# One-core attention and MLP-mixer kernel: ScalarE, VectorE and GpSimd put in written order beside TensorE, and the float64 weight conversion rearranged

## The chip, the cores and the metric

The kernel runs on one core of one Trainium2 chip. The core has five engines with an instruction stream each: PE (TensorE, matrix products), DVE (VectorE), ACT (ScalarE), POOL (GpSimd) and SP (SyncE, which here only issues DMAs). Each works through its stream in order and waits on semaphores for the others. The metric is the device time of one execution, in microseconds (us).

## The reference, cut to what matters

```
q, k, v: (8, 12, 448, 64) float32;  w_tok1 (448, 256), w_tok2 (256, 448), w_ch1 (768, 1536), w_ch2 (1536, 768) float64
q_n, k_n = rmsnorm(q, g_q), rmsnorm(k, g_k)
x  = softmax(q_n k_n^T / 8) v                    # per batch and head, then heads side by side: (8, 448, 768)
u  = x + (relu(x^T w_tok1) w_tok2)^T
out = u + relu(u w_ch1) w_ch2
```

The four weights arrive as float64. No engine operation used here reads float64, so the kernel loads each number as two 32-bit words and builds the float32 value itself.

## The kernel before, in words

Work goes by head pairs: 8 batches of 6 pairs, 48 in all. An attention step is half a pair: `score` (4 products of 448 columns into the four `s_ps` buffers, 4 exponentials on ACT that write `e`), `av` of the step before, and in the first half of a pair `denominator` of the pair before (a product with `one_c`, then transpose `dt`, reciprocal `rc`, transpose `rd`, product `uT` on DVE). `chunk_sums` adds up `e` over the keys: on POOL in a pair's first half, two additions on DVE in its second. `norm_pair` (square on ACT, `ms` on DVE, the power `rs` on POOL) and `scale` (POOL) prepare the pair two ahead; `trans_qk` (PE transposes, ACT eviction to `qkT`) the pair one ahead; `load_qk` loads three ahead.

The MLP of a batch is `trans_x`, `tok1`, `tok2`, `ch1`, `ch2`, `trans_y`. All its products, the transposes and the denominators share the two PSUM buffers of `m_ps`. The tiles `x` and `y` share one buffer, so the first `x` of a batch waits until the output DMA of the batch before has read `y`.

A weight chunk is 256 columns of 128 (or 112) rows of float64; there are 8 of the token weights, 36 of w_ch1 and 36 of w_ch2, 80 in all. Its conversion, by the lines of the profile: `raw` is loaded (L129, SP); DVE cuts out exponent (L151, to `e_t`) and mantissa (L152, to `m_t`); POOL clamps and rebases the exponent in two operations (L154, L155); ACT makes the mantissa a number (L156); DVE adds the low word (L172) and the sign (L174); POOL multiplies the two into the weight (L176, `wc_sb` or `w_sb`).

`merge` interleaves lists of items by their costs. The first stretch of the program holds 14 attention steps (the seven pairs 0 to 6) with chunk items 0 to 14. Then comes a stretch for each batch: its MLP merged with 12 attention steps of the batch after, and in the stretch of batch 0 also chunk items 15 to 80. The first stretch is called A here, that of batch 0 B. The last batch has no attention beside it.

Only PE runs in the order in which this program writes its instructions. The streams of the other engines are ordered by a scheduler, which may move an instruction ahead of others that are written before it.

Of the kernel before, what the change touches and what calls it, by code (L numbers as in the profile page):

```python
# [8 lines left out]
F32 = mybir.dt.float32  # L9
# [3 lines left out]
AF = mybir.ActivationFunctionType  # L13
ALU = mybir.AluOpType
# [26 lines left out]
def whole(ctx, tc, shifted, pre, q, k, v, g_q, g_k, moe_w_tok1, moe_w_tok2, moe_w_ch1, moe_w_ch2, out):  # L41


    nc = tc.nc
    ctx.enter_context(tc.manual_schedule(engines={nc.tensor.engine}))

    B, H, S, D = q.shape
    C = H * D
# [14 lines left out]
    SCALE = 1.0 / float(D) ** 0.5  # L63
# [18 lines left out]
    ident, one_c = pre.ident, pre.one_c
    g_t = const.tile([P, 2], F32, name="g_t")
    for i, g in enumerate((g_q, g_k)):
        for a in range(2):
            nc.scalar.dma_start(out=g_t[a * D:(a + 1) * D, i:i + 1], in_=g.rearrange("(p o) -> p o", o=1))
    nc.vector.tensor_scalar(g_t[:, 0:1], g_t[:, 0:1], SCALE, None, ALU.mult)
# [36 lines left out]
    def weight_load(i):  # L124
        rows, src, dst, split = chunks[i]
        n = src.shape[-1]
        if src.dtype == I64:
            t = raw_pool.tile([P, WCOLS, 2], U32, name="raw")
            nc.sync.dma_start(  # L129
                out=t[0:rows, 0:n, :].rearrange("p n w -> p (n w)"), in_=src.bitcast(U32))  # L130
            st["raw", i] = t
        elif split:
            t = raw_pool.tile([P, WCOLS], F32, name="raw")
            nc.sync.dma_start(out=t[0:rows, 0:n], in_=src)
            st["raw", i] = t
        else:
            nc.sync.dma_start(out=dst, in_=src)

    def convert_first(i):

        rows, src, dst, split = chunks[i]
        n = src.shape[-1]
        if src.dtype != I64:
            return
        hi = st["raw", i][0:rows, 0:n, 1]
        e_t = cv_pool.tile([P, WCOLS], U32, name="e_t")
        m_t = cv_pool.tile([P, WCOLS], U32, name="m_t")
        st["cv", i] = e_t, m_t
        e, m = e_t[0:rows, 0:n], m_t[0:rows, 0:n]
        ef, mf = e.bitcast(F32), m.bitcast(F32)  # L150
        nc.vector.tensor_scalar(e, hi, 0x7FF00000, None, ALU.bitwise_and)  # L151
        nc.vector.tensor_scalar(m, hi, 0x000FFFFF, None, ALU.bitwise_and)  # L152

        nc.gpsimd.tensor_scalar(ef, e, 1151.0 * 2**20, 896.0 * 2**20, ALU.min, ALU.max)  # L154
        nc.gpsimd.tensor_scalar(e, ef, -896.0 * 2**20, 8.0, ALU.add, ALU.mult)  # L155
        nc.scalar.activation(out=mf, in_=m, func=AF.Identity, bias=one_c[0:rows, 0:1], scale=2.0**-20)  # L156

    def convert_last(i):
# [16 lines left out]
            out=e, in0=hi, scalar=0x80000000, in1=e, op0=ALU.bitwise_and, op1=ALU.bitwise_or)  # L175
        nc.gpsimd.tensor_tensor(out=dst, in0=fold(mf), in1=fold(ef), op=ALU.mult)  # L176

    LOADS_AHEAD = 2

    def weight_items(lo, hi):  # L180

        def one(i):
            if i + LOADS_AHEAD < len(chunks):
                weight_load(i + LOADS_AHEAD)
            if i < len(chunks):
                convert_first(i)
# [302 lines left out]
class Start:  # L489


    def __init__(self, ctx, tc, q, k):
# [33 lines left out]

    def norm_pair(self, p, st, apart=False):
# [6 lines left out]
        st["rs", p] = rs = self.st_pool.tile([128, 2 * n], F32, name="rs")  # L534
# [15 lines left out]
def kernel(  # L550
# [29 lines left out]
    pre = Start(ctx, tc, q, k)  # L580
# [35 lines left out]
```

## Time and profile before

| | us |
|---|---|
| median of 3 runs | 1734.93 (1734.03 to 1735.23) |
| the profiled execution, its own time | 1736.05 |
| its span in the trace | 1734.2 |
| PE busy (matrix products) | 1558.9, 90% of the span |
| DVE busy | 490.7, 28% |
| ACT busy | 465.0, 27% |
| POOL busy | 447.6, 26% |

The span runs from the first instruction to the last; 1.85 us of the execution lie around it. Busy shares are means over the whole span, and the stretches A and B differ from the rest, so the rows further down are taken by stretch.

### The profile page before, as it was taken

The page shows a single profiled execution, that of the slowest core. Times are in us where ns is not written, and L with a number is a line of the kernel's source. Part 1 is how long each engine was busy: PE and PEld are TensorE (multiplying, and loading weights), DVE is VectorE, ACT ScalarE, POOL GpSimd, SP SyncE. Part 2 cuts the span into 40 slices and gives each one's busy share as a digit, 9 for nine tenths or more (in the row PEclk, how much of TensorE's full clock was granted, in tenths as well). Part 3 has the DMA queues.
Part 4 walks back from the last instruction along what each step waited for, and adds up shares of the span by engine and source line. Part 5 has one row for each costly group of instructions (what it writes and reads, how often), then busy time and mean ns, then how long its engine had stood idle before and what let it go on. Part 6 is the DMA issues. An engine that isn't in the chain of part 4 may idle for free.

```text
span 1734.2 us, 13947 instructions
## 1 busy us (share of the span) xinstructions
PE 1558.9 (90%) x5248; PEld 740.4 (43%) x5248; DVE 490.7 (28%) x831; ACT 465.0 (27%) x810; POOL 447.6 (26%) x393
## 2 busy tenths in 40 slices
PE   5576659999999899998999899998999989998998
PEld 2223224444444444444444444444444444444554
DVE  5867893212212221222122221122212221111000
ACT  4453333222222223222222222222222222221000
POOL 7878883111211111211121112121112111200000
PEclk8778979999999899998999999998999989999999
DMA  4333431020001100111100200011010111001001
GB/s 115 99 106 98 114 113 28 16 54 21 22 16 43 33 21 24 26 32 32 27 22 16 59 20 18 21 43 32 16 27 22 32 32 27 22 1 32 0 0 33
DMA packets 119889, 65.76 MB, mean 38 GB/s; under 512 B 91716, under 2 KB 109892, under 8 KB 119812
## 3 DMA queue, kind: packets, MB, share of 16 engines
q1 hardware_dynamic: 112066, 53.76, 11.9%
q10 hardware_dynamic: 7746, 11.01, 2.1%
q8 instruction: 43, 0.70, 0.2%
q14 instruction: 34, 0.28, 0.1%
HBM read 53.74 MB, written 11.01 MB: 37 GB/s over the span
## 4 chain that ended last, share of the span: by engine, by line
PE 79%; POOL 6%; DVE 6%; DMA 3%; ACT 2%; issue 2%; SPq 1%; ACTq 0%; DVEq 0%; POOLq 0%
PE m_ps L419 26%; PE m_ps L406 25%; PE s_ps L231 8%; PE o_ps L288 8%; PE m_ps L382 5%; PE m_ps L390 4%; DMA qk<-in_k_dram 2%; PE m_ps L302 2%; PE m_ps L216 2%; POOL rs L544 1%; POOL wc_sb L176 1%; SPq L524 1%; POOL e_t L154 1%; DMA raw<-in_moe_w_ch_dram 1%; DVE uT L424 1%
## 5 line engine op out<-in xcount | busy, mean ns | idle before, releaser
L406 PE MATMUL m_ps<-uT,wc_sb 128*128 128x448 f32 x1152 | 452.9, 547 | 26.9 <-ACT h L410 17.3
L419 PE MATMUL m_ps<-h,wc_sb 128*128 128x448 f32 x1152 | 452.4, 544 | 6.7 <-DVE uT L424 5.5
L544 POOL TENSOR_TENSOR rs<-ms,mhalf_c 112x16 f32<-112x16 f32 (+1 forms) x49 | 140.4, 2866 | 981.2 <-DVE ms L543 980.6
L406 PEld LDWEIGHTS m_ps<-uT,wc_sb 128*128 128x128 f32 x1152 | 215.5, 191 | 248.0 <-issue 206.9
L419 PEld LDWEIGHTS m_ps<-h,wc_sb 128*128 128x128 f32 x1152 | 212.8, 190 | 220.1 <-issue 207.0
L237 ACT ACTIVATE e<-s_ps,rs 112x448 f32<-112x448 f32 x384 | 213.5, 633 | 177.7 <-PE s_ps L231 174.5
L231 PE MATMUL s_ps<-qkT 64*112 64x448 f32 x768 | 184.1, 594 | 16.5 <-ACT qkT L218 11.6
L278 DVE TENSOR_TENSOR es<-es,e 112x896 f32<-112x896 f32 x96 | 105.5, 1099 | 287.8 <-ACT e L237 283.8
L288 PE MATMUL o_ps<-e,vt 112*64 112x448 f32 x768 | 171.1, 568 | 0.0
L539 DVE TENSOR_REDUCE ms<-sq 112x16 f32<-112x1024 f32 (+1 forms) x49 | 58.5, 1196 | 293.2 <-ACT sq L536 293.2
L410 ACT ACTIVATE h<-m_ps 128x448 f32<-128x448 f32 x96 | 51.9, 541 | 308.0 <-PE m_ps L406 308.0
L218 ACT ACTIVATE qkT<-m_ps,g_t 128x448 f32<-128x448 f32 x96 | 60.6, 633 | 221.7 <-PE m_ps L216 217.9
L274 POOL TENSOR_TENSOR es<-e 112x896 f32<-112x896 f32 x48 | 100.2, 2087 | 73.9 <-PE m_ps L302 73.3
L424 DVE TENSOR_TENSOR uT<-uT,m_ps 128x448 f32<-128x448 f32 x48 | 29.8, 620 | 309.3 <-PE m_ps L419 309.3
L231 PEld LDWEIGHTS s_ps<-qkT 64*112 64x112 f32 x768 | 65.7, 182 | 116.8 <-issue 89.0
L382 PE MATMUL m_ps<-x,w_sb 112*128 112x384 f32 x256 | 97.7, 540 | 10.0 <-DVE dt L314 9.5
L216 PE MATMUL m_ps<-ident,qk 112*128 112x112 f32 x384 | 57.1, 278 | 49.5 <-POOL qk L207 40.7
L288 PEld LDWEIGHTS o_ps<-e,vt 112*64 112x64 f32 x768 | 47.9, 140 | 116.0 <-issue 114.7
L390 PE MATMUL m_ps<-w_sb,h 128*128 128x448 f32 x192 | 79.8, 558 | 12.2 <-DVE uT L395 12.2
L433 ACT COPY y<-m_ps 112x512 f32<-112x512 f32 x48 | 28.0, 586 | 221.9 <-PE m_ps L431 221.9
L536 ACT ACTIVATE sq<-qk 112x1024 f32<-112x1024 f32 (+1 forms) x49 | 50.7, 1037 | 119.7 <-DMA qk<-in_k_dram 118.5
L216 PEld LDWEIGHTS m_ps<-ident,qk 112*128 112x128 f32 x384 | 46.3, 150 | 84.8 <-issue 38.9
(41 smaller groups left out, 873.1 us busy)
## 6 DMA issues: line engine op xcount, KB each, us to landing
raw<-in_moe_w_ch_dram SPq DMA_DIRECT2D x72, 256.0 KB, 2.8
qk<-in_q_dram SPq DMA_DIRECT2D x96, 112.0 KB, 2.8
qk<-in_k_dram SPq DMA_DIRECT2D x96, 112.0 KB, 2.9
vt<-in_v_dram SPq DMA_DIRECT2D x48, 224.0 KB, 2.6
out_dram<-y ACTq DMA_DIRECT2D x16, 672.0 KB, 4.6
raw<-in_moe_w_tok_dram SPq DMA_DIRECT2D x4, 224.0 KB, 4.3
raw<-in_moe_w_tok_dram SPq DMA_DIRECT2D x2, 256.0 KB, 2.6
raw<-in_moe_w_tok_dram SPq DMA_DIRECT2D x2, 192.0 KB, 2.3
```

The lines of the kernel that those rows point to most:

```text
L216: nc.tensor.transpose(ps[:, c * R:(c + 1) * R], qk[0:R, i, c].rearrange("p h d -> p (h d)"), ident[0:R, 0:R])
L218: nc.scalar.mul(st["qkT", p][:, i, :], ps[:, 0:S], g_t[:, i:i + 1])
L231: nc.tensor.matmul(out=ps[0:R, 0:S], lhsT=qkT[a * D:(a + 1) * D, 1, kc * R:(kc + 1) * R], rhs=qkT[a * D:(a + 1) * D, 0, :], start=True, st ...
L237: nc.scalar.activation(out=e[0:R, a, i, :], in_=pss[a][0:R, 0:S], func=AF.Exp, scale=st["rs", p][0:R, r:r + 1])
L274: nc.gpsimd.tensor_tensor(out=es[0:R], in0=e[0:R, :, 0, :], in1=e[0:R, :, 1, :], op=ALU.add)
L278: nc.vector.tensor_tensor(out=es[0:R], in0=es[0:R], in1=e[0:R, :, i, :], op=ALU.add)
L288: nc.tensor.matmul(out=o[a * D:(a + 1) * D, 0:S], lhsT=vt[0:R, a, kc * D:(kc + 1) * D], rhs=e[0:R, a, i, :], start=(kc == 0), stop=(kc == ...
L382: nc.tensor.matmul(out=ps[:, 0:HC], lhsT=w1_sb[0:R, c, jc * P:(jc + 1) * P], rhs=st["x"][0:R, c, cs], start=(c == 0), stop=(c == NS - 1))
L390: nc.tensor.matmul(out=ps[:, 0:S], lhsT=st["h1", jc][:, cc * P:(cc + 1) * P], rhs=w2_sb[:, jc].rearrange("p c r -> p (c r)"), start=(jc == ...
L406: nc.tensor.matmul(out=ps[:, 0:S], lhsT=wc1_sb[:, cc, f * P:(f + 1) * P], rhs=st["uT", b][:, cc, :], start=(cc == 0), stop=(cc == NC - 1))
L419: nc.tensor.matmul(out=ps[:, 0:S], lhsT=wc2_sb[:, f, cc * P:(cc + 1) * P], rhs=st["h2"][:, f, :], start=(f == 0), stop=(f == NF - 1))
L544: nc.gpsimd.tensor_tensor(out=rs[0:R, w], in0=ms[0:R, w], in1=self.mhalf_c[0:R].to_broadcast([R, (hi - lo) * n]), op=ALU.pow)
```

## The change

All four compute engines are put in written order. The clamp and rebasing of the exponent, two POOL operations, become one ACT operation, `Relu(8 x + bias)` with the bias from `expo_c`; ACT has it ahead of the mantissa's operation. In a chunk's item the load now stands last and fetches three chunks ahead instead of two. `chunk_sums` becomes an item of its own, with cost 1.0, after the step's products. The q and k of pairs 0 and 1 are loaded into the buffer that later takes w_ch2 (`wc2_sb`), so the three buffers of `qk_pool` start with pair 2; the k of pair 0 is issued on ACT's queue instead of SP's; the gains `g_t` are loaded and scaled before the branch.

```diff
-    ctx.enter_context(tc.manual_schedule(engines={nc.tensor.engine}))
+    ctx.enter_context(tc.manual_schedule(engines={
+        e.engine for e in (nc.tensor, nc.vector, nc.scalar, nc.gpsimd)}))
...
-        nc.gpsimd.tensor_scalar(ef, e, 1151.0 * 2**20, 896.0 * 2**20, ALU.min, ALU.max)
-        nc.gpsimd.tensor_scalar(e, ef, -896.0 * 2**20, 8.0, ALU.add, ALU.mult)
+        nc.scalar.activation(out=e, in_=e, func=AF.Relu, bias=expo_c[0:rows, 0:1], scale=8.0)
         nc.scalar.activation(out=mf, in_=m, func=AF.Identity, bias=one_c[0:rows, 0:1], scale=2.0**-20)
...
-    LOADS_AHEAD = 2
+    LOADS_AHEAD = 3
...
         def one(i):
-            if i + LOADS_AHEAD < len(chunks):
-                weight_load(i + LOADS_AHEAD)
             if i < len(chunks):
                 convert_first(i)
             if i:
                 convert_last(i - 1)
+            if i + LOADS_AHEAD < len(chunks):
+                weight_load(i + LOADS_AHEAD)
...
                 (score_shifted if shifted else score)(p, h)
-                chunk_sums(p, h)
...
-        items.append((4.4 - 0.8 * h, tiled))
+        items.append((3.4 - 0.8 * h, tiled))
+        if g < NG:
+            items.append((1.0, lambda: chunk_sums(p, h)))
...
+        self.wc2_sb = const.tile([P, NF, C], F32, name="wc2_sb")
+        flat = self.wc2_sb[:].rearrange("p f c -> p (f c)")
+        for p in range(2):
+            self.st["qk", p] = flat[:, 2 * p * n:2 * (p + 1) * n].rearrange(
+                "p (i c h d) -> p i c h d", i=2, c=self.NS, h=2)
-        self.load_qk(0, self.st)
+        self.load_qk(0, self.st, other=nc.scalar)
         self.load_qk(1, self.st)
```

How the streams move is shown at two places. The first is ACT in stretch A, one head pair. `e` is an exponential, `sq` the square of `norm_pair`, `qkT` the eviction of the transposes; `m_t` and `e_t` belong to a chunk. Before:

```order
L237 ACTIVATE e<-s_ps,rs 112x448
L156 ACTIVATE m_t<-m_t,one_c 128x256
L237 ACTIVATE e<-s_ps,rs 112x448 x3
L536 ACTIVATE sq<-qk 112x1024
L156 ACTIVATE m_t<-m_t,one_c 128x256
L237 ACTIVATE e<-s_ps,rs 112x448 x3
L156 ACTIVATE m_t<-m_t,one_c 128x256
L237 ACTIVATE e<-s_ps,rs 112x448
L218 ACTIVATE qkT<-m_ps,g_t 128x448 x2
L156 ACTIVATE m_t<-m_t,one_c 128x256
```

After:

```order
L233 ACTIVATE e<-s_ps,rs 112x448 x4
L553 ACTIVATE sq<-qk 112x1024
L151 ACTIVATE e_t<-e_t,expo_c 128x192
L152 ACTIVATE m_t<-m_t,one_c 128x192
L233 ACTIVATE e<-s_ps,rs 112x448 x4
L214 ACTIVATE qkT<-m_ps,g_t 128x448 x2
L151 ACTIVATE e_t<-e_t,expo_c 128x256
L152 ACTIVATE m_t<-m_t,one_c 128x256
```

The four exponentials of a step now stand together, a pair has two chunks in place of about four, and a chunk has two ACT operations that follow each other.

The same place on DVE, after the change; `es` are the additions of `chunk_sums`, `dt` to `uT` the denominator, `ms` of `norm_pair`.

```order
L274 TENSOR_TENSOR es<-es,e 112x896 x2
L148 TENSOR_SCALAR e_t<-raw 128x256
L149 TENSOR_SCALAR m_t<-raw 128x256
L168 SCALAR_TENSOR_TENSOR m_t<-raw,m_t 128x192
L170 SCALAR_TENSOR_TENSOR e_t<-raw,e_t 128x192
L310 STREAM_TRANSPOSE dt<-m_ps 128x448
L312 RECIPROCAL rc<-dt 128x14
L314 STREAM_TRANSPOSE rd<-rc 128x448
L316 TENSOR_TENSOR uT<-o_ps,rd 128x448
L556 TENSOR_REDUCE ms<-sq 112x16
L560 TENSOR_SCALAR ms<-ms 112x16
```

Before, the rows of a pair there mix about four chunks between the same attention rows:

```order
L539 TENSOR_REDUCE ms<-sq 112x16
L314 STREAM_TRANSPOSE dt<-m_ps 128x448
L543 TENSOR_SCALAR ms<-ms 112x16
L151 TENSOR_SCALAR e_t<-raw 128x256
L316 RECIPROCAL rc<-dt 128x14
L152 TENSOR_SCALAR m_t<-raw 128x256
L318 STREAM_TRANSPOSE rd<-rc 128x448
L278 TENSOR_TENSOR es<-es,e 112x896
L320 TENSOR_TENSOR uT<-o_ps,rd 128x448
L278 TENSOR_TENSOR es<-es,e 112x896
```

A chunk's first two operations now stand behind the additions, or behind the denominator and `ms`, that are written ahead of them.

The second place is POOL in stretch B. `rs` is the power, `qk` the scaling. Before:

```order
L544 TENSOR_TENSOR rs<-ms,mhalf_c 112x16
L155 TENSOR_SCALAR e_t<-e_t 128x256
L207 TENSOR_TENSOR qk<-qk,rs 112x512
L176 TENSOR_TENSOR wc_sb<-m_t,e_t 128x256
L154 TENSOR_SCALAR e_t<-e_t 128x256
L155 TENSOR_SCALAR e_t<-e_t 128x256
L176 TENSOR_TENSOR wc_sb<-m_t,e_t 128x256
L154 TENSOR_SCALAR e_t<-e_t 128x256
L155 TENSOR_SCALAR e_t<-e_t 128x256
```

After:

```order
L561 TENSOR_TENSOR rs<-ms,mhalf_c 112x16
L203 TENSOR_TENSOR qk<-qk,rs 112x512
L172 TENSOR_TENSOR wc_sb<-m_t,e_t 128x256 x11
L270 TENSOR_TENSOR es<-e 112x896
L172 TENSOR_TENSOR wc_sb<-m_t,e_t 128x256 x2
```

Of a chunk only the product is left on POOL, and a pair of stretch B has 12 or 13 of them.

## Rows read from the trace of the kernel before

**Rows 1.** Busy time by engine in stretches: start, A, B in two parts, two later batches
```profile
core 0: us, PE busy (x) PEld busy (x) DVE busy (x) ACT busy (x) POOL busy (x), PEclk, DMA share, GB/s
0.00:12.80 12.80, 0.00 (x0) 0.01 (x1) 3.20 (x11) 3.49 (x4) 5.08 (x11) 1.00 0.64 144
12.80:140.40 127.60, 83.01 (x305) 32.63 (x305) 89.82 (x184) 60.67 (x110) 106.00 (x119) 0.77 0.35 99
140.40:265.30 124.90, 80.85 (x255) 37.75 (x255) 105.06 (x214) 44.42 (x86) 106.61 (x149) 0.83 0.39 110
265.30:386.20 120.90, 118.19 (x404) 55.85 (x402) 25.90 (x38) 30.91 (x54) 24.14 (x13) 1.00 0.10 25
386.20:586.50 200.30, 190.18 (x657) 90.66 (x657) 43.50 (x63) 53.26 (x91) 35.93 (x18) 0.98 0.11 28
...
1189.60:1390.90 201.30, 191.77 (x659) 91.25 (x657) 43.69 (x63) 53.41 (x91) 35.94 (x18) 0.97 0.11 28
```

**Rows 2.** The chain that ended last, one pair of A: start, length, what
```profile
108.80 0.62 SPq L524
109.52 3.43 DMA raw<-in_moe_w_ch_dram
...
119.81 2.46 POOL qk L207
```

**Rows 3.** PE's timeline, end of A: start, length, operation, [idle before, releaser]
```profile
105.02 1.76 PE L216 MATMUL m_ps<-ident,qk 112*128 112x112 f32 x8 [5.05 <-POOL qk L207]
...
122.31 1.62 PE L216 MATMUL m_ps<-ident,qk 112*128 112x112 f32 x8 [5.00 <-POOL qk L207]
124.66 3.33 PE L231 MATMUL s_ps<-qkT 64*112 64x448 f32 x8 [0.73 <-ACT qkT L218]
...
130.15 0.92 PE L302 MATMUL m_ps<-es,one_c 112*64 112x448 f32 x4
131.00 1.76 PE L231 MATMUL s_ps<-qkT 64*112 64x448 f32 x8
132.69 1.72 PE L288 MATMUL o_ps<-e,vt 112*64 112x448 f32 x8
```

**Rows 4.** Groups by line in 0:260 us: a chunk's operations on POOL and ACT
```profile
L176 POOL TENSOR_TENSOR wc_sb<-m_t,e_t 128x256 f32<-128x256 f32 x69 | 59.3, 862 | 15.2 <-DVE e_t L174 10.5 <-DVE m_t L172 1.1
...
L154 POOL TENSOR_SCALAR e_t<-e_t 128x256 f32<-128x256 uint32 x72 | 40.5, 563 | 11.4 <-DVE e_t L151 6.1
...
L156 ACT ACTIVATE m_t<-m_t,one_c 128x256 f32<-128x256 uint32 x72 | 36.5, 507 | 94.1 <-DVE m_t L152 93.2
...
L155 POOL TENSOR_SCALAR e_t<-e_t 128x256 uint32<-128x256 f32 x72 | 34.7, 482 | 6.0
```

**Rows 5.** Groups by line, 600:1000 us, two later batches: attention's operations
```profile
L237 ACT ACTIVATE e<-s_ps,rs 112x448 f32<-112x448 f32 x96 | 52.9, 635 | 47.9 <-PE s_ps L231 47.9
...
L278 DVE TENSOR_TENSOR es<-es,e 112x896 f32<-112x896 f32 x24 | 26.2, 1092 | 90.8 <-ACT e L237 89.6
...
L218 ACT ACTIVATE qkT<-m_ps,g_t 128x448 f32<-128x448 f32 x24 | 15.2, 633 | 61.3 <-PE m_ps L216 61.3
L539 DVE TENSOR_REDUCE ms<-sq 112x16 f32<-112x1024 f32 x12 | 14.6, 1220 | 90.7 <-ACT sq L536 90.7
...
L536 ACT ACTIVATE sq<-qk 112x1024 f32<-112x1024 f32 x12 | 12.7, 1055 | 39.6 <-DMA qk<-in_k_dram 39.6
...
L314 DVE STREAM_TRANSPOSE dt<-m_ps 128x448 f32<-128x448 f32 x12 | 7.8, 650 | 35.8 <-PE m_ps L302 35.8
```

**Rows 6.** DVE's timeline in A: two of a chunk's four operations, undisturbed
```profile
85.33 0.41 DVE L174 SCALAR_TENSOR_TENSOR e_t<-raw,e_t 128x256 uint32<-128x256 uint32 x1
85.66 0.28 DVE L151 TENSOR_SCALAR e_t<-raw 128x256 uint32<-128x256 uint32 x1
```

**Rows 7.** The scaling's group in 600:1000 us
```profile
L207 POOL TENSOR_TENSOR qk<-qk,rs 112x512 f32<-112x512 f32 x12 | 12.5, 1042 | 0.9
```

**Rows 8.** Waits in 600:1000 us: total us, times, longest
```profile
PE m_ps L367 <- DVE x L374: 11.5, 4, 5.3
```

More of the change, by code (lines that the diff above doesn't have):

```diff
@@ L62, in whole @@
     assert DT % P == 0 and C % P == 0 and DC % P == 0 and HC <= 512 and S <= 512
-    SCALE = 1.0 / float(D) ** 0.5
     pool = lambda name, bufs, **kw: ctx.enter_context(tc.tile_pool(name=name, bufs=bufs, **kw))
@@ L68, in whole @@
     cv_pool = pool("cv_pool", 3)
+    pre.qk_pool = pool("qk_pool", 3)
+    pre.sq_pool = pool("sq_pool", 1)
+    pre.st_pool = pool("st_pool", 4)
     v_pool = pool("v_pool", 2)
@@ L80, in whole @@
     ps_M = pool("ps_M", 2, space=PSUM)
[L82 to L87, printed above, removed]
+    ident, one_c, expo_c, g_t = pre.ident, pre.one_c, pre.expo_c, pre.g_t
     w1_sb = const.tile([P, NS, DT], F32, name="w1_sb")
@@ L91, in whole @@
     wc1_sb = const.tile([P, NC, DC], F32, name="wc1_sb")
-    wc2_sb = const.tile([P, NF, C], F32, name="wc2_sb")
+    wc2_sb = pre.wc2_sb
     st = dict(pre.st)
@@ L149, in convert_first @@
         e, m = e_t[0:rows, 0:n], m_t[0:rows, 0:n]
-        ef, mf = e.bitcast(F32), m.bitcast(F32)
+        mf = m.bitcast(F32)
         nc.vector.tensor_scalar(e, hi, 0x7FF00000, None, ALU.bitwise_and)
         nc.vector.tensor_scalar(m, hi, 0x000FFFFF, None, ALU.bitwise_and)
-        nc.gpsimd.tensor_scalar(ef, e, 1151.0 * 2**20, 896.0 * 2**20, ALU.min, ALU.max)
-        nc.gpsimd.tensor_scalar(e, ef, -896.0 * 2**20, 8.0, ALU.add, ALU.mult)
+        nc.scalar.activation(out=e, in_=e, func=AF.Relu, bias=expo_c[0:rows, 0:1], scale=8.0)
         nc.scalar.activation(out=mf, in_=m, func=AF.Identity, bias=one_c[0:rows, 0:1], scale=2.0**-20)
@@ L489, with __init__ @@
 class Start:
-    def __init__(self, ctx, tc, q, k):
+    def __init__(self, ctx, tc, q, k, g_q, g_k, w2):
         self.nc = nc = tc.nc
@@ L500, in __init__ @@
         const = pool("start", 1)
-        self.qk_pool = pool("qk_pool", 3)
-        self.sq_pool = pool("sq_pool", 1)
-        self.st_pool = pool("st_pool", 4)
+        NF, C = w2.shape[0] // P, w2.shape[1]
+        self.wc2_sb = const.tile([P, NF, C], F32, name="wc2_sb")
+        n = 2 * self.NS * D
+        flat = self.wc2_sb[:].rearrange("p f c -> p (f c)")
+        assert NF * C >= 4 * n
         self.st = {}
-        self.load_qk(0, self.st)
+        for p in range(2):
+            self.st["qk", p] = flat[:, 2 * p * n:2 * (p + 1) * n].rearrange(
+                "p (i c h d) -> p i c h d", i=2, c=self.NS, h=2)
+        self.load_qk(0, self.st, other=nc.scalar)
         self.load_qk(1, self.st)
+        self.g_t = const.tile([P, 2], F32, name="g_t")
+        for i, g in enumerate((g_q, g_k)):
+            for a in range(2):
+                nc.scalar.dma_start(
+                    out=self.g_t[a * D:(a + 1) * D, i:i + 1], in_=g.rearrange("(p o) -> p o", o=1))
         self.mhalf_c = const.tile([P, 1], F32, name="mhalf_c")
         nc.gpsimd.memset(self.mhalf_c[:], -0.5)
-        self.norm_pair(0, self.st, apart=True)
         self.ident = const.tile([P, P], F32, name="ident")
@@ L513, in __init__ @@
         nc.gpsimd.memset(self.one_c[:], 1.0)
+        self.expo_c = const.tile([P, 1], F32, name="expo_c")
+        nc.gpsimd.memset(self.expo_c[:], -896.0 * 2**23)
+        self.st["rs", 0] = const.tile([P, 4 * self.NS], F32, name="rs_0")
+        with tc.tile_pool(name="sq_0", bufs=1) as self.sq_pool, tc.tile_pool(name="st_0", bufs=1) as self.st_pool:
+            self.norm_pair(0, self.st, apart=True)
+        nc.vector.tensor_scalar(self.g_t[:, 0:1], self.g_t[:, 0:1], 1.0 / float(D) ** 0.5, None, ALU.mult)
     def heads(self, p):
@@ L517, in heads, with load_qk @@
         return b, slice(2 * j, 2 * j + 2)
-    def load_qk(self, p, st):
+    def load_qk(self, p, st, other=None):
         b, hs = self.heads(p)
-        st["qk", p] = qk = self.qk_pool.tile([128, 2, self.NS, 2, self.D], F32, name="qk")
+        if ("qk", p) not in st:
+            st["qk", p] = self.qk_pool.tile([128, 2, self.NS, 2, self.D], F32, name="qk")
+        qk = st["qk", p]
         for i, src in enumerate((self.q, self.k)):
             for a in range(2):
-                self.nc.sync.dma_start(
+                (other if other and i else self.nc.sync).dma_start(
                     out=qk[0:self.R, i, :, a], in_=src[b, hs][a].rearrange("(p c) d -> p c d", c=self.NS))
@@ L533, in norm_pair @@
         ms = self.st_pool.tile([128, 2 * n], F32, name="ms")
-        st["rs", p] = rs = self.st_pool.tile([128, 2 * n], F32, name="rs")
+        if ("rs", p) not in st:
+            st["rs", p] = self.st_pool.tile([128, 2 * n], F32, name="rs")
+        rs = st["rs", p]
         for lo, hi in ((0, 1), (1, 2)) if apart else ((0, 2),):
@@ L579 @@
     nc.vector.tensor_scalar(small[:], most[:], SCORE_BOUND**2 / D, None, ALU.is_le)
-    pre = Start(ctx, tc, q, k)
+    pre = Start(ctx, tc, q, k, g_q, g_k, moe_w_ch2)
     with tc.If(nc.values_load(small[0:1, 0:1], min_val=0, max_val=1,
```

## The prediction

> **What bounds the kernel now.** I read the busy times by stretch first [rows 1]. In the five later batches (200.3 to 201.3 us, the first and last are shown) PE is busy for 190.2 to 191.8 us: they are bound by PE, and about 6 of the remaining 10 us are the wait of `trans_x` for the output DMA, 11.5 us in two batches [rows 8]. The first 265 us are different. PE is busy for 83.0 of 127.6 us in A and 80.9 of 124.9 us in the first part of B, at a granted clock of 0.77 and 0.83, while POOL is busy for 106.0 and 106.6 us. From 265.3 us on, with the conversions done, B runs like a later batch (118.2 of 120.9 us, clock 1.00). So there are some 90 us in which PE doesn't work, and more in which it works at the lower of its two levels (1.2 in place of 2.4 GHz), all before 265 us.
>
> The chain of waits shows what a pair of A waits for: a `raw` DMA of 3.43 us, behind it on SP's queue the q and k of a later pair (0.62 us an issue), then `ms`, the power and the scaling on POOL (2.46 us) [rows 2]; PE gets its next transposes after 5.0 us of idling for `qk`, 17.3 us after those of the pair before [rows 3]. The scheduler has put about four chunks into each pair of A, and SP, which issues in order, reaches the q and k only when the chunks ahead have given their `raw` buffers back. In B, POOL alone carries 1.91 us a chunk (0.86 + 0.56 + 0.48 [rows 4]).
>
> **Stretch A after the change.** It keeps 14 steps and has 15 chunk items, as written: two chunks a pair, not four. The loads of q and k stand behind at most one raw load each and find the three buffers of the pool empty at first, so they come a pair early; I cost them at nothing, covered by a whole pair's time (without that cover the price is the present chain, a rival below). What is left is the engines' own work and the order. ACT has, per pair, 8 exponentials of 0.635, a square of 1.06, two evictions of 0.63 [rows 5] and 2.14 chunks with two operations of about 0.51 (the new `Relu` is on the same 128x256, so I price it as L156 [rows 4]): 5.1 + 1.1 + 1.3 + 2.2 = 9.6 us. PE at full clock has 2 x (1.76 + 1.72) + 0.92 + 1.6 = 9.5 us [rows 3]. POOL has a sixth of a later batch's 35.9 us, 6.0 [rows 1], and 2.14 products of 0.86: 7.8 us.
>
> The written order adds a loop between ACT and DVE. Half 0: four exponentials (2.5), the square (1.06), on DVE `ms` (1.22) and the first cut of a chunk (0.28 [rows 6]), then on ACT the chunk's two operations (1.0): 6.1 us. Until then the next step's exponentials, whose scores are ready, stand behind the chunk on ACT. Half 1: four exponentials (2.5), the second addition (1.09) while ACT evicts `qkT` (1.27), the cut (0.28), the chunk's two (1.0): 4.9 us. Together 11.0 us, some six handoffs between engines on top; the denominator (two transposes of 0.65 and two shorter operations) ran before that unless PE was late. PE idles in this loop, so a part of its work will run at the lower clock (the same scores took 3.33 us after 5 us of idling, 1.76 us later [rows 3]) and move the denominator into the loop. I take 12.5 us a pair, from 9.6 (ACT alone) to 17.3 (as now). A then ends at 12.8 + 7 x 12.5 = 100.3 us instead of 140.4 us.
>
> The start stays at 12.8 us [rows 1]: q of pair 0 is issued first on SP as now; k leaves on ACT's queue, which saves two issues of 0.62 us [rows 2] to a transfer that isn't needed before the second half of the square. I take 0, with 1.2 us either way.
>
> **Stretch B after the change.** It has the instructions of a later batch plus 65 chunks. PE's share is that of a later batch, 201 us less the 6 us for the output DMA (batch 0 has no `y` ahead of it): 195 us. The others beside it, each as in a later batch plus 65 chunks: DVE 43.6 + 65 x 1.38 (2 x 0.28 + 2 x 0.41 [rows 6]) = 133 us; ACT 53.3 + 65 x 1.02 = 119 us; POOL 35.9 + 65 x 0.86 = 92 us. None reaches 195 us. POOL's 65 x 1.05 = 68 us of L154 and L155 are gone; ACT pays 33 us for it, beside PE's work. The DMA has to bring 105 GB/s or so in B, against 110 GB/s at a share of 0.39 now [rows 1]; no price.
>
> What the order costs in B: an eviction that PE waits for (`uT` on DVE, `h` on ACT) can stand behind one chunk's operations, 1.4 or 1.0 us. A group of `ch1` or `ch2` gives the other `m_ps` buffer enough time; the six short groups of `tok2` don't. Also, w_ch2 chunks are now converted only just before the `ch2` columns that read them, where the scheduler had finished all 80 by 265 us; at the first, third and fifth column group PE may wait for a chunk that is one or two items late. Nothing in the trace shows this. From below it is 0; from above 30 us, if DVE's and POOL's work don't overlap at all (next part). I take 11 us, nearer to 0, since every engine alone has a third of B free. B takes 206 us and ends at 306.3 us.
>
> Why an overlap could fail: the scaling takes 2.46 us in A, where DVE is busy 70% of the time [rows 1, 2], and 1.04 us in later batches [rows 7]. The Trainium skill, page "GPSIMD Engine Reference", section "1. Specifications", says why: GpSimd shares its SBUF interfaces with VectorE and contends with instructions of two SBUF inputs or in a two-port mode. By the row only the scaling is stretched, and B stays at 206 us; by the page taken as full exclusion, B would be 236 us. The trace agrees with contention; it doesn't show exclusion.
>
> **Later batches and the end.** Their instructions stay, in another order. PE's idle time there is 10 us a batch, 6 of them the output DMA, so no order can win more than 4 us a batch; what it can lose is the last rival. I take 0.
>
> **Sum.** B now ends at 386.2 us [rows 1], then at 306.3 us: 79.9 us less. Against the profiled execution's own time, 1736.05 - 79.9 = 1656 us. That execution lies 1.1 us above the median of the runs shown, so the median should be **1655 us**.
>
> **The rivals.**
> *DVE and POOL exclude each other* (that page's rule in full). For it: the stretched scaling. Against: in A now, 89.8 + 106.0 us of the two fit into 127.6 us [rows 1], though part of that is waiting inside the operations. B = 133 + 92 + 11 = 236 us, 30 more: 1685 us. 14%.
> *A stays at its pace*: the loads come late again, or the ACT and DVE loop with the slow clock reaches 17.3 us a pair. For it: the new waits stand in order. Against: half the chunks and no raw queue. A ends at 133.9 us, 34 more: 1689 us. 13%.
> *All of it is hidden*: A goes at ACT's 9.6 us, B at 195 us: 80 + 195 = 275 us, 31 less: 1624 us. For it: no engine's sum is over PE's in B. Against: the loop in A. 11%.
> *Slower*: in each of the 72 steps of the later batches DVE holds the denominator and the additions (1.3 and 2.2 us [rows 5]) or ACT its four exponentials ahead of an eviction that PE needs. From 1.1 us a step on (79.9 / 72) the gain is gone; at 2.2 us the time is 1813 us. For it: two `m_ps` buffers only. Against: the scheduler's order there already holds whole groups of four exponentials and two additions, and PE loses under 4 us a batch. 5%.
> *No effect*: the gain of A and B is eaten by conversion waits at `ch2` to within 0.2%: 3%.
>
> **How the numbers follow.** My forecast has 54%: 12.5 us a pair by about 1.5 and B's cost between 0 and 20 us give 1637 to 1673 us by themselves. The range takes in the two rivals above it at 1685 and 1689 us with a margin, and leaves out most of the hidden case, the slower one and no effect: 1635 to 1698 us. Within 0.2% (3.5 us, about what a measurement of this kernel can tell from no change) lies 3%; slower 5%; faster 92%.
>
> **What would show it.** In the trace after: no POOL line between the scaling and the product of a chunk; PE's transposes in A every 11 to 14 us; `trans_x` of batch 0 at about 100 us and that of batch 1 at about 306 us; granted clock over 0.9 through B; the later batches at 200 to 202 us. I am wrong if the batches move by more than 2 us each, if PE in B waits over 20 us for `wc_sb`, or if the power or scaling of a pair still ends A's chain.

## The result, and the profile after

The changed kernel took 1678.42 us (median, 1674.74 to 1678.93) where the kernel before took 1734.48 us beside it: a ratio of 0.9673 [0.9656, 0.969], 56 us faster, where 80 us were forecast. The profiled execution took 1678.31 us, with a span of 1676.5 us, so its stretches can be set against those of [rows 1].

In this table (us, read from each trace) A ends with the first `trans_x` of batch 0, B with that of batch 1. "Rest" is what follows, the later batches with their tails. The rows under the first two are the experiments below.

| kernel | A starts | A ends | length of B | rest | span |
|---|---|---|---|---|---|
| before | 12.8 | 140.4 | 245.8 | 1348.0 | 1734.2 |
| after | 13.3 | 116.7 | 222.5 | 1337.3 | 1676.5 |
| Relu alone | 12.5 | 126.8 | 225.4 | 1349.0 | 1701.2 |
| all but the Relu | 13.4 | 117.4 | 246.0 | 1334.6 | 1698.0 |
| PE's item costs alone | 12.8 | 139.0 | 245.7 | 1347.6 | 1732.3 |
| a fourth `cv_pool` buffer | 13.3 | 117.7 | 221.6 | 1338.2 | 1677.5 |
| chunks at the end of a pair | 13.2 | 81.5 | 225.7 | 1336.6 | 1643.8 |
| ACT's part an item later | 13.2 | 84.3 | 218.1 | 1338.7 | 1641.1 |
| both of these | 13.3 | 81.1 | 220.2 | 1336.9 | 1638.2 |
| no power | 10.9 | 112.0 | 218.0 | 1337.8 | 1667.8 |
| no conversion in B | 13.2 | 115.1 | 195.9 | 1336.8 | 1647.8 |
| no ACT operations in B's chunks | 13.4 | 117.9 | 208.5 | 1338.5 | 1664.9 |
| no low word and sign in B's chunks | 13.4 | 114.1 | 202.4 | 1339.0 | 1655.5 |

The end of B moved by 47.0 us: 23.7 by the end of A (140.4 to 116.7) and 23.3 by B's own length (245.8 to 222.5). The rest is 10.7 us shorter. The same windows as in [rows 1] for the kernel after (A, B, a later batch; columns as there):

```profile
13.30:116.70 103.40, 72.09 (x305) 27.76 (x305) 58.71 (x111) 59.27 (x110) 59.65 (x35) 0.87 0.35 87
116.70:339.20 222.50, 200.02 (x656) 95.31 (x656) 142.25 (x327) 107.95 (x222) 100.77 (x87) 0.93 0.34 96
339.20:537.40 198.20, 188.96 (x656) 90.34 (x656) 44.52 (x63) 53.17 (x91) 36.17 (x18) 0.99 0.11 28
```

POOL is busy for 58% of A, where it was 83% before, yet PE is idle for 31 us of A's 103, and the granted clock is 0.87: part of A still runs at the lower of its two levels, 1.2 in place of 2.4 GHz. In B, PE is idle for 22.5 us.

What now spaces the pairs of A is seen in the chain that ended last, here for one of its two slowest pairs (start, length, what):

```profile
70.46 3.33 PE s_ps L227 x8
73.79 2.56 PE o_ps L284 x8
76.35 0.75 PE m_ps L298 x4
...
80.56 0.73 POOL wc_sb L172
81.30 2.04 POOL es L270
83.36 1.10 DVE es L274
...
84.56 1.09 DVE es L274
85.65 0.21 DVE e_t L148
...
85.95 0.51 ACT e_t L151
86.46 0.40 ACT m_t L152
86.86 1.05 ACT qkT L214 x2
...
87.95 3.33 PE s_ps L227 x8
```

No DMA stands in it, and neither power nor scaling, unlike [rows 2]. In this pair it is a ring around four engines: from scores (70.46) to scores (87.95) 17.5 us. The chain of waits shows who released whom; what lies between the denominator's product on PE (until 77.10) and POOL's product for a chunk (80.56) stands on DVE, in its timeline:

```profile
78.79 0.62 DVE L316 TENSOR_TENSOR uT<-o_ps,rd 128x448 f32<-128x448 f32 x1
79.33 0.28 DVE L148 TENSOR_SCALAR e_t<-raw 128x256 uint32<-128x256 uint32 x1
...
79.73 0.42 DVE L168 SCALAR_TENSOR_TENSOR m_t<-raw,m_t 128x256 f32<-128x256 uint32 x1
80.07 0.41 DVE L170 SCALAR_TENSOR_TENSOR e_t<-raw,e_t 128x256 uint32<-128x256 uint32 x1
```

The denominator ends with `uT` at 79.4 us; a chunk's operations are written behind it. POOL's product waits for the sign (L170), POOL's part of `es` stands behind that product, DVE's additions need POOL's part, the next cut stands behind the additions, ACT's two operations need the cut, and `qkT`, which the next scores need, stands behind those two. POOL's `es` is not alone there. The additions are also written behind `ms`, which ends on DVE at the same moment (82.79 + 0.57 = 83.36 us):

```profile
82.79 0.57 DVE L560 TENSOR_SCALAR ms<-ms 112x16 f32<-112x16 f32 x1
```

The chains of the pairs whose scores start at 26.6, 40.4, 54.1, 87.9 and 102.9 us don't go over POOL at all. They go through the denominator on DVE, then a cut and ACT's two operations, as in the pair that starts at 40.4 us:

```profile
45.44 0.80 PE m_ps L298 x4
...
46.26 0.66 DVE dt L310
...
48.53 1.14 DVE ms L556
...
49.77 0.27 DVE e_t L148
...
50.86 2.09 ACT e L233 x4
52.96 1.06 ACT qkT L214 x2
```

All these rings share a chunk's operations on DVE behind the denominator, ACT's two operations and `qkT`. PE's timeline has the price, here for the slowest pairs:

```profile
70.46 3.33 PE L227 MATMUL s_ps<-qkT 64*112 64x448 f32 x8 [6.33 <-ACT qkT L214]
...
77.03 1.76 PE L227 MATMUL s_ps<-qkT 64*112 64x448 f32 x8
...
87.95 3.33 PE L227 MATMUL s_ps<-qkT 64*112 64x448 f32 x8 [6.59 <-ACT qkT L214]
```

From the second pair on, PE waits for `qkT` for 2.35, 3.72, 3.61, 6.33, 6.59 and 4.25 us. Behind the three longest of these waits the scores take 3.33 us, behind the others 2.17 to 2.34 us, where they take 1.76 us at the higher clock.

### The profile page after: what moved, and what is told of

It reads as the page before. It is cut to its first block, busy times and chain, and to the rows that moved or that the text cites. A ratio compares the mean times of both kernels' runs of the same rounds, so it can differ in the third digit from the quotient of the medians.

```text
span 1676.5 us, 13714 instructions
## 1 busy us (share of the span) xinstructions
PE 1539.9 (92%) x5248; PEld 734.3 (44%) x5248; DVE 473.2 (28%) x831; ACT 493.9 (29%) x890; POOL 368.6 (22%) x234
## 4 chain that ended last, share of the span: by engine, by line
PE 83%; DVE 6%; ACT 4%; DMA 3%; POOL 2%; issue 2%; SPq 0%; ACTq 0%; DVEq 0%; POOLq 0%
PE m_ps L416 26%; PE m_ps L403 24%; PE s_ps L227 9%; PE o_ps L284 9%; PE m_ps L379 5%; PE m_ps L387 4%; PE m_ps L298 2%; DMA out_dram<-y 2%; PE m_ps L364 2%; PE m_ps L212 1%; DVE uT L421 1%; ACT qkT L214 1%; POOL rs L561 1%; PE m_ps L428 1%; DVE es L274 1%
## 5 line engine op out<-in xcount | busy, mean ns | idle before, releaser
L227 PE MATMUL s_ps<-qkT 64*112 64x448 f32 x768 | 180.0, 590 | 27.6 <-ACT qkT L214 27.6
L561 POOL TENSOR_TENSOR rs<-ms,mhalf_c 112x16 f32<-112x16 f32 (+1 forms) x49 | 144.5, 2949 | 223.7 <-DVE ms L560 216.6
L310 DVE STREAM_TRANSPOSE dt<-m_ps 128x448 f32<-128x448 f32 x48 | 31.2, 650 | 452.3 <-PE m_ps L298 452.3
L274 DVE TENSOR_TENSOR es<-es,e 112x896 f32<-112x896 f32 x96 | 113.7, 1185 | 82.5 <-ACT e L233 77.9
L172 POOL TENSOR_TENSOR wc_sb<-m_t,e_t 128x256 f32<-128x256 f32 x72 | 62.5, 875 | 123.2 <-DVE e_t L170 122.1
L379 PE MATMUL m_ps<-x,w_sb 112*128 112x384 f32 x256 | 86.9, 497 | 0.0
L364 PE MATMUL m_ps<-ident,uT 128*112 128x128 f32 x192 | 40.7, 378 | 41.7 <-ACT x L369 36.8
## 6 DMA issues: line engine op xcount, KB each, us to landing
qk<-in_q_dram SPq DMA_DIRECT2D x92, 112.0 KB, 2.8
qk<-in_k_dram SPq DMA_DIRECT2D x92, 112.0 KB, 2.8
wc_sb<-in_q_dram SPq DMA_DIRECT2D x4, 112.0 KB, 3.8
```

What stands on the lines that cost most here:

```text
L227: nc.tensor.matmul(out=ps[0:R, 0:S], lhsT=qkT[a * D:(a + 1) * D, 1, kc * R:(kc + 1) * R], rhs=qkT[a * D:(a + 1) * D, 0, :], start=True, st ...
L274: nc.vector.tensor_tensor(out=es[0:R], in0=es[0:R], in1=e[0:R, :, i, :], op=ALU.add)
L364: nc.tensor.transpose(ps[0:R, c * P:(c + 1) * P], st["uT", b][:, j, c * R:(c + 1) * R], ident[:, :])
L379: nc.tensor.matmul(out=ps[:, 0:HC], lhsT=w1_sb[0:R, c, jc * P:(jc + 1) * P], rhs=st["x"][0:R, c, cs], start=(c == 0), stop=(c == NS - 1))
L561: nc.gpsimd.tensor_tensor(out=rs[0:R, w], in0=ms[0:R, w], in1=self.mhalf_c[0:R].to_broadcast([R, (hi - lo) * n]), op=ALU.pow)
```

## The experiments

**The Relu alone, and everything but the Relu.** Two kernels part the change into its main halves. The first is the kernel before with the one edit of a chunk's exponent:

```diff
-        nc.gpsimd.tensor_scalar(ef, e, 1151.0 * 2**20, 896.0 * 2**20, ALU.min, ALU.max)
-        nc.gpsimd.tensor_scalar(e, ef, -896.0 * 2**20, 8.0, ALU.add, ALU.mult)
+        nc.scalar.activation(out=e, in_=e, func=AF.Relu, bias=expo_c[0:rows, 0:1], scale=8.0)
```

> The kernel before with one part of the change alone: the exponent's clamp and rebasing become one Relu on ACT; the scheduler still orders DVE, ACT and POOL, two loads ahead. Theory O (the gain comes from the written order, which paces the chunks and lets q and k come early): A keeps about 16 to 18 us a pair, because the chain there is raw DMA, SP's queue, q and k, power; only B gets shorter; 1700 to 1725 us. Rival R (the gain is POOL's 1.05 us a chunk): 1670 to 1685 us, as the changed kernel.

Measured: 1702.2 us, ratio 0.9807 [0.9783, 0.9832]. The second is the kernel after with the same edit turned round, so POOL clamps again.

> The changed kernel with the exponent's two operations back on POOL in place of the Relu on ACT; all else as changed. Theory O: A about as in the changed kernel (14 to 15.5 us a pair, end of A at 113 to 122 us); in B POOL has 36 + 65 x 1.91 = 160 us in order beside 195 us of PE, so B grows by 10 to 35 us; 1685 to 1715 us. Rival R: nearly all is lost, 1720 to 1735 us.

Measured: 1703.19 us, 0.9816 [0.98, 0.9833]. Its four executions spread from 1699.95 to 1704.8 us and the profiled one is the shortest, so its row in the table may be some 3 us short. Both times lie in theory O's ranges, and so do A's pace with the Relu alone (114.3 / 7 = 16.3 us a pair) and A's end and B's length without it. One sentence of the theory fails: not only B gets shorter by the Relu, A ends 13.6 us sooner too. Each half is worth some 33 us alone; together they give 56. The table says where. B's gain is the Relu's: with it alone B takes 225.4 us in the scheduler's order, and without it 246.0 us in the written order. In A the order, with the loads changed beside it, reaches all of the gain without the Relu (A ends at 117.4 us), and the Relu alone reaches 13.6 of the 23.7 us in the scheduler's order; the two don't add up there. The rest's gain is the order's: 1334.6 us without the Relu, 1349.0 us with the Relu alone. POOL in B of the kernel without it, the windows' fifth busy time:

```profile
117.40:363.40 246.00, 204.53 (x656) 97.20 (x656) 157.20 (x327) 82.65 (x157) 177.46 (x219) 0.89 0.31 87
```

177 of 246 us busy, and PE's longest wait in B for `qkT` 9.4 us, against 6.0 us in the kernel after.

**PE's item costs alone.** The split of `chunk_sums` into an item also changes the costs by which PE's own order is merged. This kernel is the one before with those costs and an empty item:

```diff
-        items.append((4.4 - 0.8 * h, tiled))
+        items.append((3.4 - 0.8 * h, tiled))
+        if g < NG:
+            items.append((1.0, lambda: None))
```

> The kernel before with nothing changed but the merge: a step's products cost 3.4 less 0.8 h and an empty item of 1.0 follows, so PE's order is that of the changed kernel, and the scheduler still orders DVE, ACT and POOL. Theory M (the later batches' 1 to 2 us come from PE's order, in which the next attention step follows the transposes of x at once): later batches at 198 to 200 us, 1720 to 1730 us in all. Rival W (they come from the written order of the other engines): later batches at 200.3 to 201.3 us, 1732 to 1738 us.

Measured: 1734.28 us, 0.9998 [0.999, 1.0007]: the rival W, no effect. In its trace PE's operations follow each other, function by function, as in the kernel after, yet the rest stays at 1347.6 us. So the 10.7 us there don't come from PE's order. The order of the other engines remains, since the edits of the loads act on the first pairs and on the chunks, which are done by then.

**A fourth buffer for a chunk's parts.** In B, DVE's cut is seen to wait for POOL's product, which frees a buffer of `cv_pool`. One edit: `cv_pool` from 3 to 4.

> The changed kernel with four buffers for e_t and m_t in place of three. Theory P (in B, POOL holds the products while it does a power and a scaling, three buffers run full, DVE and ACT stop, and an eviction that PE needs stands behind a chunk on ACT): one chunk more of slack, PE's waits for qkT and uT in B shrink, B 4 to 10 us shorter, 1668 to 1674 us. Rival C (DVE and POOL contend for SBUF, buffers don't matter): within 2 us of the changed kernel's 1678 us.

Measured: 1677.2 us, 0.9663 [0.9647, 0.9679]; B 221.6 us, the figure of rival C. DVE's waits in B for POOL's product (total us, times, longest), first in the kernel after, then with the fourth buffer:

```profile
DVE e_t L148 <- POOL wc_sb L172: 17.7, 10, 4.6
```

```profile
DVE e_t L148 <- POOL wc_sb L172: 7.9, 4, 4.6
```

The buffer takes away over half of these waits and B gains 0.9 us. Theory P falls for the buffers: the wait is there, but most of it isn't what PE waits for. Rival C's reason, contention, isn't shown by this.

**The chunks at the end of a pair.** If A's ring comes from chunks written between one step's parts, moving them out breaks it. The items of A are the same; a pair's two or three chunk items now stand behind its two steps:

```diff
-    for _, fn in merge(att_items(0, AHEAD * per + 2), weight_items(0, BEFORE)):
+    w = weight_items(0, BEFORE)
+    begin = []
+    for g in range(AHEAD * per + 2):
+        begin += att_step(g)
+        if g % 2:
+            n = (len(w) * (g + 1)) // (AHEAD * per + 2) - (len(w) * (g - 1)) // (AHEAD * per + 2)
+            begin += w[(len(w) * (g - 1)) // (AHEAD * per + 2):][:n]
+    for _, fn in begin:
         fn()
```

> The changed kernel with the chunk items of A put at the end of each pair, behind its transposes, in place of the merge by costs: two or three chunks a pair, none between the two steps. Theory L (A's pace is a loop: scores, products and denominator on PE, the denominator on DVE, a chunk's cut behind it, the chunk's two operations on ACT ahead of the next exponentials, and again ahead of qkT): the chunks leave the loop, 9.6 to 11.5 us a pair, A ends at 81 to 95 us, 1653 to 1665 us. Rival S (A's pace is the slow clock and POOL's es, the chunks only fill gaps): under 5 us gained, 1673 us or more.

Measured: 1646.82 us, 0.9493 [0.9478, 0.9509]. Theory L holds: a pair takes 9.3 to 10.4 us and A ends at 81.5 us; the whole is 6 us below its range. The windows row of A:

```profile
13.20:81.50 68.30, 61.80 (x304) 25.89 (x304) 50.93 (x99) 56.57 (x104) 56.88 (x33) 1.00 0.50 122
```

PE's timeline for one pair of it:

```profile
53.85 1.76 PE L227 MATMUL s_ps<-qkT 64*112 64x448 f32 x8 [0.87 <-ACT qkT L214]
...
63.14 1.76 PE L227 MATMUL s_ps<-qkT 64*112 64x448 f32 x8 [0.87 <-ACT qkT L214]
```

PE's waits for `qkT`, 2.35 to 6.59 us in the kernel after, are 0.86 or 0.87 us from the second pair on, the clock is 1.00, and PE's work in A fell from 72.1 to 61.8 us. No operation was left out. Some of the last chunks' operations now run behind A's end (99 on DVE in A in place of 111), and B is 3.2 us longer, so of A's 35 us the end of B keeps 32 (339.2 to 307.2 us). That is what the places of the chunks in the order alone cost.

**ACT's part of a chunk an item later.** Another way out of the ring: item i cuts chunk i on DVE, does ACT's two operations of chunk i-1, and DVE's last two and the product of chunk i-2, so no engine waits for what was written just ahead. `cv_pool` has 4 buffers for it, the loads run 2 ahead, and A has one chunk item more.

```diff
             if i < len(chunks):
                 convert_first(i)
-            if i:
-                convert_last(i - 1)
+            if 1 <= i <= len(chunks):
+                convert_act(i - 1)
+            if i >= 2:
+                convert_last(i - 2)
```

> The changed kernel with one item more between a chunk's steps: item i cuts chunk i on DVE, runs ACT's two operations of chunk i-1 and finishes chunk i-2; four buffers for e_t and m_t, two loads ahead. ACT then finds its cut already made an item ago. Theory K: ACT no longer waits for the cut that was just written, A takes 11 to 13.5 us a pair, B 205 to 215 us, 1650 to 1668 us. Rival P: A 14 us or more a pair, B 218 us or more, 1674 us or more.

Measured: 1643.44 us, 0.9472 [0.9458, 0.9487]. A's pairs take 9.3 to 10.6 us, less than theory K's 11 to 13.5. In B it wins 4.4 us only: 218.1 us is the rival's figure, not theory K's 205 to 215. So the longer distance cures A as well, but wins only a sixth of B's 26.6 us (further down). Both edits together:

> Both: the chunk items of A at the end of each pair and the longer distance between a chunk's steps. Theory K: A at 9.4 us a pair as with the chunks last alone, B 205 to 215 us, 1628 to 1640 us. Rival P: B as before, 1643 to 1650 us.

Measured: 1639.9 us, 0.9453 [0.944, 0.9467], the fastest kernel of the study, 38.5 us below the kernel after. The total is in theory K's range and A is as it has it, but B, 220.2 us, is not (205 to 215). The two edits cure the same thing in A (81.5, 84.3, 81.1 us), so they don't add up.

**No power.** `ALU.mult` stands in for the power on POOL, so the norms aren't computed.

> The changed kernel with the power of norm_pair on POOL replaced by a multiplication of the same tiles (the norms are then not computed; all else is). Theory P (in B the power and the scaling hold POOL for 4 to 6 us, products and cuts pile up behind it, and evictions behind those): PE's waits for qkT and uT in B fall under 8 us, B takes 205 to 214 us, the whole 1660 to 1670 us. Rival K (evictions wait because ACT stands in line behind DVE's cuts, whatever POOL does): B stays at 218 us or more, 1674 us or more.

Measured: 1667.97 us, 0.9612 [0.9599, 0.9626]. The operation's mean fell from 3226 to 535 ns in B, 16 us of POOL's time for six. B became 4.5 us shorter (218.0 us, the rival's figure), A started 2.4 us sooner and was 2.3 us shorter, so the total is in theory P's range though B is not (205 to 214). PE's waits for `qkT` at L212 fell from 9.0 to 4.1 us in all and the longest from 6.0 to 3.3 us, but those for `qkT` and `uT` together only from 20.0 to 14.0 us, not under 8. So the long power, with a chunk's product queued behind it, is one of B's stalls but not the main one.

**What the conversions cost in B.** In three kernels a part of the 65 chunks of B is left out, so their weights are wrong: the whole conversion (loads stay, POOL fills the weight with a constant), ACT's two operations, or DVE's last two (low word and sign).

```diff
-        if src.dtype != I64:
+        if src.dtype != I64 or i >= BEFORE:
             return
...
+        if i >= BEFORE:
+            nc.gpsimd.memset(dst, 0.01)
+            return
```

> The changed kernel in which the 65 chunks of B are loaded but not converted (a fill of the weight's columns by POOL stands in place of the seven operations, so DVE and ACT have no chunk in B); A is unchanged. Theory V (all that B takes beyond a later batch is evictions waiting behind chunks, and the lower clock that these waits bring): B takes 194 to 202 us, PE waits in it under 8 us, the clock is 0.97 or more. Rival F (batch 0's stretch is slow by itself, by its merge or its start from the lower clock): B takes 210 us or more.

Measured: 1649.04 us, 0.9515 [0.9487, 0.9542], from two executions; B 195.9 us, as theory V has it. The windows row of B:

```profile
115.10:311.00 195.90, 190.63 (x657) 91.15 (x657) 46.53 (x67) 53.25 (x92) 57.62 (x87) 0.98 0.34 103
```

Without ACT's two operations:

```diff
+        if i >= BEFORE:
+            return
         nc.scalar.activation(out=e, in_=e, func=AF.Relu, bias=expo_c[0:rows, 0:1], scale=8.0)
```

> The changed kernel, without ACT's two operations (Relu and the mantissa's) for the 65 chunks of stretch B; DVE's four and POOL's product stay, and the weights that they give are wrong. Stretch B takes 222.5 us in the changed kernel and 195.9 us where none of the 65 is converted; the 26.7 us between are what the conversions cost. Theory N (it is the place of ACT between DVE and DVE: evictions such as qkT stand on ACT behind two operations that wait for DVE's cuts, and DVE's additions of the next item wait for ACT): most of the 26.7 us goes with the ACT operations, B is 197 to 207 us, and PE's waits for qkT (9.0 us in all) go; time 1653 to 1663 us. Theory D (it is DVE's load: uT and the additions of e stand behind four operations of 1.4 us a chunk, and POOL's stretch beside them): B stays at 214 to 222 us; time 1670 to 1678 us.

Measured: 1665.02 us, 0.959 [0.9574, 0.9606]; B 208.5 us. Its windows row:

```profile
117.90:326.40 208.50, 196.45 (x657) 93.75 (x657) 143.13 (x327) 53.31 (x92) 99.82 (x87) 0.95 0.35 102
```

Without DVE's last two:

```diff
-        nc.vector.scalar_tensor_tensor(
+        if i < BEFORE:
+            nc.vector.scalar_tensor_tensor(
```

> The changed kernel, without DVE's two last operations of a chunk (low word and sign) for the 65 chunks of stretch B; the cuts, ACT's two and POOL's product stay, so the weights lack the low word and the sign. Theory N (ACT's place between DVE and DVE): the cuts still stand ahead of ACT, so qkT still waits; B is 214 to 222 us; time 1670 to 1678 us. Theory D (DVE's load): two of the four DVE operations, 0.82 of 1.38 us a chunk, are gone, and over half of the 26.7 us with them; B is 200 to 210 us; time 1656 to 1666 us. If neither of this run and the one without ACT's operations takes B below 214 us, the cost lies in no single engine.

Measured: 1657.34 us, 0.9553 [0.9537, 0.9569]; B 202.4 us. Its windows row:

```profile
114.10:316.50 202.40, 193.88 (x656) 92.36 (x656) 85.73 (x197) 106.49 (x222) 93.83 (x87) 0.97 0.35 105
```

All conversions together cost 222.5 - 195.9 = 26.6 us. Of that 9.4 us is PE's own work (200.0 against 190.6 us for the same matrix products, at a clock of 0.93 against 0.98), and 17.2 us is idling (22.5 against 5.3 us). ACT's two operations are worth 14.0 us, DVE's last two 20.1 us. Theory D named the range of the second run rightly, but neither theory did for the first, and the two parts, 34.1 us, sum to more than the whole. So they remove in part the same stalls: PE's waits for `qkT` at its transposes, 9.0 us in all in the kernel after, fall to 0.7 us in both runs, also in the second, where theory N had them stay. That fits a chain of cut, ACT, DVE and POOL in fixed order, of which either link can be taken out. It doesn't clear the engines' load, since each run takes load and links away together, and the later ACT part, which changes the chain and not the load, won 4.4 us only.

## Why the forecast was right, and which terms were mis-sized

**The start** was taken at 12.8 us with 1.2 us either way; it is 13.3.

**Stretch A, the term 12.5 us a pair: mis-sized.** The mean is 103.4 / 7 = 14.8 us, so A ends at 116.7 instead of 100.3 us. What the forecast said of the loads came true: no `raw` DMA is in the chain. ACT's price was right too (the Relu takes 0.51 us). (PE's sum of 9.5 us was a little too high: its 1.6 us for the transposes are rows behind 5 us of idling, and in the kernel after they take 0.99 us. It bounded nothing.) The loop was drawn too small. The forecast summed half 0 and half 1 on ACT and DVE to 11.0 us and put the denominator outside "unless PE was late"; it also mentioned the lower clock, with 1.5 us for all of it. PE is late from the second pair on: the chains there go through the denominator, except in the pair of 17.5 us, and there the chunk is cut right behind it. That pair's ring holds PE's scores, products and the denominator's product at the lower clock (70.46 to 77.10, 6.6 us), DVE's denominator (2.3 us), the end of a chunk on DVE and its product on POOL (to 81.30, 1.9 us), POOL's `es` (2.04 us), and then the half that the forecast had: additions, cut, ACT's two, `qkT`. POOL's `es` was in no term of the loop, but it sets the pace in this pair alone, and there beside `ms`. Moving the chunks out of the ring brings A to 9.3 to 10.4 us a pair and the clock from 0.87 to 1.00, which shows that the pace was the order's doing, the lower clock included.

**The rival "A stays at its pace"** (17.3 us a pair) was half true: two of the seven pairs took 17.2 and 17.3 us, the others 9.9 to 14.3. Of its two mechanisms the loop of ACT and DVE with the slow clock is the right one, with the denominator in it; its price held for two pairs.

**Stretch B, the floor of 195 us: right.** Without conversions B takes 195.9 us, though it was worked out only from a later batch less the wait for the output DMA.

**Stretch B, the term of 11 us for the order: mis-sized**, it is 26.6 us, within the bounds of 0 and 30. Two things were left out. First, the forecast let an eviction wait for one chunk's operations, 1.4 us; it can wait for a whole chain, as around 250 us in the kernel after:

```profile
243.02 4.84 POOL rs L561
...
247.93 1.04 POOL qk L203
248.97 0.69 POOL wc_sb L172
...
249.69 0.81 DVE e_t L148
...
250.52 0.51 ACT e_t L151
...
251.43 2.09 ACT e L233 x4
...
254.35 0.42 DVE m_t L168
...
257.56 0.29 DVE e_t L148
...
257.88 0.51 ACT e_t L151
...
258.78 0.53 ACT qkT L214
...
259.36 1.01 PE m_ps L212 x4
```

The eviction `qkT` needs nothing of this; it is behind a chunk on ACT, which waits for a cut on DVE, which is behind the additions, and so on back to a power of 4.84 us. PE lost 6.02 us there, the longest of its waits in B. Second, 9.4 of the 26.6 us is PE working at the lower clock after such stalls, which had no term at all. PE's waits in B by releaser (total us, times, longest):

```profile
PE m_ps L212 <- ACT qkT L214: 9.0, 3, 6.0
PE m_ps L428 <- DVE uT L421: 5.4, 2, 5.1
PE m_ps L387 <- DVE uT L392: 4.6, 2, 2.4
```

These are evictions on DVE and ACT, as the forecast said; its fear that PE would wait at `ch2` for `wc_sb` didn't come true, no row names it.

**The rival that DVE and POOL exclude each other** gave B 236 us. In B the two are busy for 142.3 + 100.8 = 243 us of 222.5, but waiting can lie inside an operation, so the sum alone doesn't settle it. The timeline does, for the power:

```profile
143.77 2.90 POOL L561 TENSOR_TENSOR rs<-ms,mhalf_c 112x16 f32<-112x16 f32 x1 [0.61 <-DVE ms L560]
...
144.05 0.41 DVE L168 SCALAR_TENSOR_TENSOR m_t<-raw,m_t 128x256 f32<-128x256 uint32 x1
...
243.02 4.83 POOL L561 TENSOR_TENSOR rs<-ms,mhalf_c 112x16 f32<-112x16 f32 x1
```

Inside the first of these powers seven of DVE's operations of a chunk run, the one shown among them. They take 0.28 to 0.42 us each, where undisturbed ones take 0.28 and 0.41 [rows 6], and the power takes the 2.90 us that it takes in later batches. So there is no exclusion here. The Trainium skill, page "GPSIMD Engine Reference", section "1. Specifications", names contention of the two engines for their shared SBUF interfaces, not exclusion. The trace agrees in that some operations are stretched: three powers of A, with DVE's two additions beside them, take 3.75 to 3.78 us. It doesn't show that contention is the reason, and another with additions over its last 2 us takes 2.90. The power's mean of 3226 ns in B, against 2904 ns in later batches, is the work of one: five of the six take 2.90 or 2.91 us, four of them with eight of DVE's operations of a chunk beside them, and the one of 4.83 us has the same eight beside it.

**The rival that all of it is hidden** fell with the 26.6 us of B and A's 14.8 us; A at 9.4 us a pair, its first half, is what moving the chunks reached.

**Later batches at 0: wrong by 10.7 us.** The forecast capped what order could win at 4 us a batch and took nothing; six batches win 1.3 to 2.8 us each, 1.8 in the mean. It had named a move of over 2 us each as a sign of being wrong, and two of the six are over it. The two profiles differ at `trans_x`. Before, PE's group from 586.47 to 598.58 us (12.1 us) is cut in three behind its first wait, and ACT and DVE have `sq` and `ms` of the next norm between the copies of `x`:

```profile
593.45 1.06 ACT L536 ACTIVATE sq<-qk 112x1024 f32<-112x1024 f32 x1 [6.24 <-DMA qk<-in_k_dram]
594.41 0.57 ACT L372 COPY x<-m_ps 112x512 f32<-112x512 f32 x1
```

After, the written order holds the copies together, and the group takes 10.2 us (to 547.6):

```profile
537.44 1.44 PE L364 MATMUL m_ps<-ident,uT 128*112 128x128 f32 x8
543.77 3.84 PE L364 MATMUL m_ps<-ident,uT 128*112 128x128 f32 x16 [4.90 <-ACT x L369]
```

These two groups differ most. Over the six batches the groups take 69.3 us before and 61.8 after, so 7.5 of the 10.7 us are won at `trans_x`; the other 3.2 us weren't located. That it is the order of ACT, DVE and POOL follows from two runs (PE's order alone wins nothing, the kernel without the Relu wins it in full); that `trans_x` is the place is read from the rows, not tried by itself.

**Sum.** -23.7 in A and the start where -40.1 was forecast, -23.3 in B for -39.8, -10.7 in the rest for 0: 57.7 us of the profiled spans against 79.9. The direction and both mechanisms, the conversion off POOL and the loads off A's path, hold; the two loops across engines were priced too low, by 32.9 us together. That the time lies only 22 us from the forecast is owed in part to luck: the 10.7 us of the later batches, put at nothing, made up for a third of it.

**Open.** Which of the load edits (w_ch2's buffer for the first pairs, k on ACT's queue, three chunks ahead) A's gain needs wasn't parted from the order, nor why the Relu alone brings A's end forward by 13.6 us. The one power of 4.83 us in B is as long in the kernels with the chunks at the end of a pair and with ACT's part later; what holds it isn't shown. In the fastest kernel, B is still 24 us above the kernel without conversions; the fourth buffer, the later ACT part and the power took 0.9, 4.4 and 4.5 us of the like, and the remainder wasn't settled.

## What to carry to other kernels

When several engines run in written order, price a pair of work not by each engine's sum but by the ring: follow from one use of a result back to the engine's own last use, through every operation that is written ahead on each engine, needed or not. A helper task that goes back and forth between engines (here DVE, ACT, DVE, POOL) belongs behind the steps that PE waits for, or with its stages an item apart; here that was worth another 38 us, nearly all of it in A. Where PE idles in such a ring for several microseconds, as here, count its own work ahead of the next handoff at the lower clock.

## What the hardware showed unexpectedly

In the kernel after, with waits of 2.35 to 6.59 us for `qkT` ahead of a pair's scores, A's mean granted clock was 0.87 and its 305 matrix products took 72.1 us. With waits of 0.87 us the clock was 1.00 and 304 of them took 61.8 us. And a chunk's operations on DVE didn't set the length of POOL's power: four powers of B with eight of DVE's operations of a chunk beside them took 2.90 or 2.91 us, a fifth with the same eight beside it 4.83 us. That one, with a chunk's product queued behind it, stood at the head of PE's longest wait in B.
